# Pooled attention and a cosine-gated feed-forward: one unit order in the steady stages, and the cut of the last 128 rows

## The chip, the core and the metric

The kernel runs on one core of a Trainium2 chip. The metric is the device time of one execution in microseconds (us), as a median over runs. TensorE (PE, its weight loads listed apart as PEld) multiplies, VectorE (DVE) multiplies and copies out of PSUM, ScalarE (ACT) does exp, ln and sine, GpSimd (POOL) pools keys and values, SyncE (SP) issues DMAs.

## The reference

`q`, `k`, `v` are 8 x 8 x 576 x 64 (batch, heads, sequence, head size), `x` has 4608 tokens of 512, `w_in` is 512 x 2048, `w_out` 2048 x 512.

```python
k_p = k.reshape(B, H, 72, 8, D).mean(axis=3); v_p = likewise
attn = softmax(q @ k_p.T / sqrt(D))          # 72 pooled keys
x = (attn @ v_p) with heads side by side     # 4608 x 512
h = x @ w_in; g = h * cos(h); out = g @ w_out
```

## The kernel before

The feed-forward runs in nine stages `t` of 512 tokens. A stage is an **up phase** (64 matmuls of N=512 at L297, eight pairs of PSUM banks in turn, pair `fp` in `banks[fp % 3]`; ScalarE takes the cosine, VectorE multiplies into `g_sb`) and a **down phase** (64 matmuls of N=512 at L310 in four row blocks `ms` of 16, in `obanks[ms % 2]`; after each block `down_out` copies it to an `o_sb` buffer at L316 and issues two DMAs at L320). There are three `o_sb` buffers in rotation.

The attention of batch `b = t + 1` is done inside the down phase of stage `t`, by hand: a list `fill` of (place, step), where the step is issued ahead of down matmul number `place`. Engines work in the order of issue. A batch's 576 columns are cut into four units `us[0..3]` of 256 columns by four heads, and a rest, `REST`, of 64 columns and eight heads. A unit has two steps, each using one of the three pairs `banks[0..2]`:

- `scores` (matmuls at L211, then one exp on ScalarE at L218 into a tile `ex`); `two_` issues the matmuls of two units, then their exps.
- `values` (matmuls at L241; then on ScalarE two Ln of half the partitions each at L247 and one Exp at L248, which writes `inv`; then two multiplies on VectorE at L252, which write `xT`).

In the stages t = 1 to 6, which the text calls steady, `fill` places the four units of batch t+1 and the rest of batch t. The rest's columns are needed by the next up phase: its first matmul, at L297, reads `xT` and waits for the last multiply of L252. Before and after the ScalarE work of a down phase the activation tables are switched (L285, L288).

The last 128 rows (t = 8, ms = 3) are done by `last_chunk`, after everything else: 16 matmuls for each column piece, each piece copied and sent out by two DMAs of 64 rows, one from SP's queue and one from ACT's.

Of the kernel before, what the change touches and what calls it, by code (L numbers as in the profile page):

```python
# [19 lines left out]
def kernel(  # L20
# [9 lines left out]
    nc = tc.nc  # L30
    B, H, S, D = q.shape
# [15 lines left out]
    REST = (SEG[2], (0, H))  # L47
# [14 lines left out]
    w_out_sb = [wpool.tile([128, 4, d_model], BF16, name=f"w_out_sb{i}") for i in range(4)]  # L62
# [9 lines left out]
    banks = [psum.tile([128, 2, 512], FP32, name=f"bank{i}") for i in range(3)]  # L72
# [34 lines left out]
    def load_q(b):  # L107
        q_tile(b)
        load_even(staged["q", b], b, q)
# [60 lines left out]
    def k_transpose(b):  # L170
        nc.sync.dma_start_transpose(out=kk[b % 2], in_=kp2[b % 2].rearrange("p h s d -> p (h s d)"))
# [10 lines left out]
    def q_transpose(b):  # L182
        qT_tile(b)
        nc.sync.dma_start_transpose(out=att["qT", b], in_=q_flat(b))
# [10 lines left out]
    def ex_col(u, i):  # L195

        (c0, n), (h0, nh) = u
        return (i // 2 % 2 * (nh // 2) + i // 4 * 2 + i % 2) * n

    def scores(b, u, pair):  # L200
        scores_mm(b, u, pair)
        scores_exp(b, u, pair)

    def scores_mm(b, u, pair):
        (c0, n), (h0, nh) = u

        for i in [i + 2 * a for k in range(0, nh, 4) for i in (k, k + 1) for a in range(2)]:
            bank, c = divmod(ex_col(u, i), nh * n // 2)
            pj, hp = divmod(h0 + i, 2)
            g, r = divmod(ROW * pj + ORDER[c0 // 64], 2)  # L210
            nc.tensor.matmul(pair[:Sp, bank, c:c + n].rearrange("p (g n) -> p g n", n=64),  # L211
                             lhsT=kk[b % 2][half[r], h0 + i, 0:Sp],
                             rhs=att["qT", b][half[r], g:g + n // 64, hp * 64:hp * 64 + 64])

    def scores_exp(b, u, pair):
        (c0, n), (h0, nh) = u
        ex = asb.tile([Sp, 4 * 256], BF16, name="ex", tag="ex", bufs=EX)
        nc.scalar.activation(out=ex[:, 0:nh * n].rearrange("p (a n) -> p a n", a=2), in_=pair[:Sp, :, 0:nh * n // 2],  # L218
                             func=ACTF.Exp, scale=scale / POOL)
        att["ex", b, u] = ex  # L220

    def x_out(b, u, rows):
        (c0, n), (h0, nh) = u
        return xT[rows, h0 // 2:(h0 + nh) // 2, b * S + c0:b * S + c0 + n]

    def cols(x, u):
        n = u[0][1]
        return x[:, 0:n * u[1][1] // 2].rearrange("p (j n) -> p j n", n=n)

    def inverse_tile(w):  # L230
        lnc = asb.tile([128, 512], FP32, name="lnc", tag="lnc", bufs=1)
        inv = asb.tile([128, 512], FP32, name="inv", tag="inv", bufs=3)
        return lnc[:, 0:w], inv[:, 0:w]

    def values(b, u, pair, later=None):

        (c0, n), (h0, nh) = u
        ex = att.pop(("ex", b, u))
        for i in range(nh):
            pj, hp = divmod(h0 + i, 2)  # L240
            nc.tensor.matmul(pair[:, hp, (i // 2) * n:(i // 2 + 1) * n],  # L241
                             lhsT=vz[b % 2][:, pj, 2 * hp:2 * hp + 2, :].rearrange("p a d -> p (a d)"),
                             rhs=ex[:, ex_col(u, i):ex_col(u, i) + n])
        w = nh * n // 2
        lnc, inv = inverse_tile(w)
        for hp in range(2):
            nc.scalar.activation(out=lnc[half[1 - hp]], in_=pair[half[1 - hp], hp, 0:w], func=ACTF.Ln)  # L247
        nc.scalar.activation(out=inv, in_=lnc, func=ACTF.Exp, scale=-1.0)  # L248

        def mul():  # L250
            for hp in range(2):
                nc.vector.tensor_mul(out=x_out(b, u, half[hp]), in0=cols(pair[half[hp], hp, :], u),  # L252
                                     in1=cols(inv[half[1 - hp]], u))

        if later is None:
            mul()
        else:
            later.append(mul)
# [54 lines left out]
    def down_out(t, ms, ps, c0=0, queues=(nc.sync, nc.sync)):  # L313
        o = msb.tile([128, d_model], FP32, name="o_sb", tag="o_sb")
        n = ps.shape[1]
        nc.vector.tensor_copy(out=o[:, 0:n], in_=ps)  # L316
        rows_of = out.rearrange("(b p t) m -> b t p m", b=B, t=ROW)
        for i, rows in enumerate(half):
            b_, pos = divmod((t * TILE + ms * 128) // 64 + i, ROW)
            queues[i].dma_start(out=rows_of[b_, ORDER[pos], :, c0:c0 + n], in_=o[rows, 0:n])  # L320

    def last_chunk():

        t, ms = NT - 1, 3
        for hc in range(2):
            ps = banks[hc][:, 0, 0:256]
            for fc in range(FFCH):
                nc.tensor.matmul(ps, lhsT=g_sb[:, fc, ms * 128:(ms + 1) * 128],  # L328
                                 rhs=w_out_sb[fc // 4][:, fc % 4, hc * 256:(hc + 1) * 256],
                                 start=(fc == 0), stop=(fc == FFCH - 1))  # L330
            down_out(t, ms, ps, hc * 256, (nc.sync, nc.scalar))


    EX = 5
# [90 lines left out]
    for t in range(NT):  # L425
        b = t + 1
        for fp in range(FFCH // 2):
            up_mm(t, fp, 2 if t == 0 and fp < 2 else 0)
            between = ()
            if t == 0:  # L430
                if fp == 4:
                    puts = pool_k_mm(1, obanks[0], 0, 2), pool_k_mm(1, obanks[1], 2, 4)
                elif fp in (5, 6):
                    g0 = 9 * (fp - 5)
                    puts = q_transpose_mm(1, obanks[0], g0, g0 + 5), q_transpose_mm(1, obanks[1], g0 + 5, g0 + 9)
                if fp in (4, 5, 6):
                    puts[0](vec)
                    between = ((puts[1], act),)
            up_g(t, fp, between)
            if 0 < t and b < B:  # L440
                if fp == 0:
                    q_transpose(b)
                elif fp == 2:
                    k_transpose(b)
        mms = [(ms, fc) for ms in range(4) for fc in range(FFCH)]
        if t == 0:
            mms = [(ms, fc) for hm in range(2) for cg in range(4) for ms in range(2 * hm, 2 * hm + 2)
                   for fc in range(4 * cg, 4 * cg + 4)]


        def S_(n, bank):
            return lambda: scores(b, us[n], banks[bank])

        later = []

        def V_(n, bank, wait=None):
            return lambda: values(b, us[n], banks[bank], wait)

        fill = []
        if t < B:  # L460
            exp_tables()
            late = 0 < t and b < B
            fill = [(1, lambda: scores(t, REST, banks[2])), (12, lambda: values(t, REST, banks[2 if late else 1]))]
        if t == 0:
            fill[1:] = [(2, S_(0, 0)), (8, lambda: pool_v_mm(1, banks[1])), (8, lambda: values(t, REST, banks[2])),
                        (11, S_(1, 0)), (13, V_(0, 1)), (18, S_(2, 2)), (21, V_(1, 0, later)), (26, S_(3, 1)),
                        (32, lambda: later.pop()()), (32, V_(2, 2)), (40, V_(3, 0))]
        elif b < B:
            us = BY_TOKENS


            def two_(n, bank0, bank1):
                def go():
                    for mm in (scores_mm, scores_exp):
                        mm(b, us[n], banks[bank0])
                        mm(b, us[n + 1], banks[bank1])
                return go

            fill = [(4, two_(0, 2, 0)), (14, V_(0, 1)), (19, V_(1, 2)), (32, two_(2, 0, 1)), (36, fill[0][1]),
                    (38, V_(2, 0)), (41, V_(3, 1)), (45, fill[1][1])]  # L480
        fi = 0
        if t == NT - 1:
            mms = mms[:-FFCH]
        for n, (ms, fc) in enumerate(mms):
            while fi < len(fill) and fill[fi][0] <= n:
                fill[fi][1]()
                fi += 1
            down_mm(obanks[ms % 2], ms, fc)
            if fc == FFCH - 1:
                down_out(t, ms, obanks[ms % 2])  # L490
        if t < B:
            sin_tables()
        if 0 < t and b + 1 < B:

            nc.gpsimd.tensor_copy(out=gate, in_=kk[b % 2][0:1, 0, 0:1])  # L495
        if b + 1 < B:
            load_kv(b + 1, "k", k)
            load_q(b + 1)
            load_kv(b + 1, "v", v)
            pool_add(b + 1, "k")  # L500
            pool_add(b + 1, "v")
# [29 lines left out]
```

## Time and profile before

| | us |
|---|---|
| median of 3 runs (303.58 to 303.91) | 303.9 |
| the profiled execution | 303.9 |
| its span, first to last instruction | 302.1 |
| PE busy, 1798 matmuls | 294.0 |
| ACT busy | 206.8 |
| DVE busy | 172.3 |

The profiled execution's time is that of the median; 1.8 us of it lie around the span. The granted TensorE clock is full in all 40 slices of the span. The chain of work that ended last, followed back from the end, is 85% PE. Rows of the tail: `L328 PE MATMUL ... 128x256 bf16 x32` 273 ns each, `L316 DVE COPY o_sb<-bank 128x256` 424 ns, `L316 DVE COPY o_sb<-obank 128x512` 689 ns, DMAs of 64 KB 1.9 us (SP) and 2.2 us (ACT) from issue to landing, of 128 KB 2.4 us.

A time in the text such as 138.76 is in us from the span's start. A line of the timeline gives start, length, engine, source line, what is written and read, the count of merged instructions, and in brackets the idle time ahead of them and who ended it. In the chain a piece starts where the one before it ended, so a matmul's start there is up to 0.17 us later than the instruction's own.

### The profile page before, as it was taken

The page shows a single profiled execution, that of the slowest core. Times are in us where ns is not written, and L with a number is a line of the kernel's source. Part 1 is how long each engine was busy: PE and PEld are TensorE (multiplying, and loading weights), DVE is VectorE, ACT ScalarE, POOL GpSimd, SP SyncE. Part 2 cuts the span into 40 slices and gives each one's busy share as a digit, 9 for nine tenths or more (in the row PEclk, how much of TensorE's full clock was granted, in tenths as well). Part 3 has the DMA queues.
Part 4 walks back from the last instruction along what each step waited for, and adds up shares of the span by engine and source line. Part 5 has one row for each costly group of instructions (what it writes and reads, how often), then busy time and mean ns, then how long its engine had stood idle before and what let it go on. Part 6 is the DMA issues. An engine that isn't in the chain of part 4 may idle for free.

```text
span 302.1 us, 4605 instructions
## 1 busy us (share of the span) xinstructions
PE 294.0 (97%) x1798; PEld 141.6 (47%) x1798; DVE 172.3 (57%) x211; ACT 206.8 (68%) x255; POOL 129.8 (43%) x92
## 2 busy tenths in 40 slices
PE   8799999999999999999999999999999999999995
PEld 3545544445544454455444544454444544444444
DVE  5558636574566366645675566656574567425712
ACT  3887897469856986688768876788578956606500
POOL 8553007984973596349733991399100000000000
PEclk9999999999999999999999999999999999999999
DMA  7999999639546943695169617881900330131032
GB/s 152 201 207 206 208 204 196 152 44 174 109 113 105 167 92 70 123 171 113 44 132 161 115 36 162 129 141 36 167 5 1 71 69 0 27 79 35 0 71 71
DMA packets 44006, 32.92 MB, mean 109 GB/s; under 512 B 22096, under 2 KB 39248, under 8 KB 43984
## 3 DMA queue, kind: packets, MB, share of 16 engines
q0 software_dynamic: 19744, 18.07, 38.2%
q1 hardware_dynamic: 24080, 14.42, 21.0%
q8 instruction: 14, 0.23, 0.3%
q10 hardware_dynamic: 160, 0.13, 0.2%
q14 instruction: 8, 0.07, 0.1%
HBM read 36.70 MB, written 9.44 MB: 153 GB/s over the span
## 4 chain that ended last, share of the span: by engine, by line
PE 85%; DMA 10%; POOL 2%; ACT 1%; issue 0%; DVE 0%; POOLq 0%; ACTq 0%
PE obank L310 39%; PE bank L297 37%; DMA w_out_sb<-in_moe_w_out_dram 6%; PE bank L241 5%; DMA w_in_sb<-in_moe_w_in_dram 4%; PE bank L211 3%; PE bank L328 1%; POOL kv_st L84 1%; POOL kp L384 1%; POOL q_b L84 1%; ACT L285 0%; ACT cos L304 0%; ACT ex L218 0%; POOL identity masks.py:197 0%; DVE o_sb L316 0%
## 5 line engine op out<-in xcount | busy, mean ns | idle before, releaser
L310 PE MATMUL obank<-w_out_sb,g_sb 128*128 128x512 bf16 x560 | 132.5, 380 | 0.5 <-DMA w_out_sb<-in_moe_w_out_dram 0.5
L297 PE MATMUL bank<-xT,w_in_sb 128*128 128x512 bf16 x576 | 126.5, 379 | 0.0
L304 ACT ACTIVATE cos<-bank,half_pi 128x1024 f32<-128x1024 f32 x72 | 80.0, 1113 | 63.3 <-PE bank L297 63.3
L307 DVE TENSOR_TENSOR g_sb<-bank,cos 128x1024 bf16<-128x1024 f32 x72 | 88.1, 1225 | 48.2 <-ACT cos L304 48.2
L297 PEld LDWEIGHTS <-w_in_sb 128*128 128x128 bf16 x576 | 55.5, 98 | 68.6 <-DVE xT L252 2.5
L310 PEld LDWEIGHTS <-g_sb 128*128 128x128 bf16 x560 | 52.2, 97 | 56.9 <-issue 3.7
L252 DVE TENSOR_TENSOR xT<-bank,inv 64x512 bf16<-64x512 f32 (+1 forms) x72 | 45.3, 629 | 50.1 <-ACT inv L248 49.2
L141 POOL TENSOR_TENSOR kv_st<-kv_st 72x2048 f32<-72x2048 bf16 x12 | 48.7, 4056 | 35.2 <-DMA kv_st<-in_k_dram 35.2
L247 ACT ACTIVATE lnc<-bank 64x512 f32<-64x512 f32 (+1 forms) x72 | 39.2, 544 | 2.9 <-PE bank L241 1.3
L218 ACT ACTIVATE ex<-bank 72x1024 bf16<-72x1024 f32 (+1 forms) x40 | 35.0, 928 | 5.3 <-PE bank L211 5.2
L316 DVE COPY o_sb<-obank 128x512 f32<-128x512 f32 x35 | 23.6, 689 | 16.8 <-PE obank L310 16.2
L142 POOL TENSOR_TENSOR kv_st<-kv_st 72x1024 f32<-72x1024 f32 x12 | 28.2, 2348 | 1.0
L248 ACT ACTIVATE inv<-lnc 128x512 f32<-128x512 f32 (+1 forms) x36 | 21.0, 583 | 1.1
L241 PE MATMUL bank<-ex,vz 72*128 72x256 bf16 (+1 forms) x176 | 20.0, 243 | 0.2 <-ACT ex L218 0.2
L241 PEld LDWEIGHTS <-vz 72*128 72x128 bf16 x176 | 13.7, 97 | 9.9 <-issue 0.6
L145 POOL TENSOR_TENSOR kp<-kv_st 72x512 bf16<-72x512 f32 x12 | 14.9, 1264 | 0.5
L211 PE MATMUL bank<-qT,kk 64*72 64x256 bf16 (+1 forms) x192 | 13.3, 252 | 1.1 <-ACT qT L193 0.5
L211 PEld LDWEIGHTS <-kk 64*72 64x72 bf16 x192 | 7.6, 110 | 11.9 <-issue 8.1
L285 ACT ACT_TABLE_LOAD x9 | 11.5, 1283 | 0.9 <-PEq L515 0.7
L288 ACT ACT_TABLE_LOAD x9 | 11.5, 1283 | 0.2
L495 POOL COPY gate<-kk 1x1 bf16<-1x1 bf16 x5 | 0.9, 180 | 24.7 <-DMA kk<-kp 24.7
L84 POOL DMA_DIRECT2D q_b<-in_q_dram x10 | 7.7, 773 | 2.7 <-DMA w_in_sb<-in_moe_w_in_dram 1.4
(55 smaller groups left out, 89.8 us busy)
## 6 DMA issues: line engine op xcount, KB each, us to landing
out_dram<-o_sb SPq DMA_DIRECT2D x70, 128.0 KB, 2.4
kv_st<-in_v_dram POOLq DMA_DIRECT2D x8, 576.0 KB, 13.0
kv_st<-in_k_dram POOLq DMA_DIRECT2D x7, 576.0 KB, 7.7
q_b<-in_q_dram POOLq DMA_DIRECT2D x6, 576.0 KB, 9.9
w_in_sb<-in_moe_w_in_dram POOLq DMA_DIRECT2D x4, 512.0 KB, 13.7
w_out_sb<-in_moe_w_out_dram POOLq DMA_DIRECT2D x4, 512.0 KB, 18.4
q_b<-in_q_dram POOLq DMA_DIRECT2D x4, 288.0 KB, 12.1
g_sb<-in_k_dram SPq DMA_DIRECT2D x1, 576.0 KB, 3.5
```

The lines of the kernel that those rows point to most:

```text
L141: add(out=s, in0=x[:, :, 0:4, :], in1=x[:, :, 4:8, :], op=ADD)
L142: add(out=s[:, :, 0:2, :], in0=s[:, :, 0:2, :], in1=s[:, :, 2:4, :], op=ADD)
L211: nc.tensor.matmul(pair[:Sp, bank, c:c + n].rearrange("p (g n) -> p g n", n=64), lhsT=kk[b % 2][half[r], h0 + i, 0:Sp], rhs=att["qT", b][h ...
L218: nc.scalar.activation(out=ex[:, 0:nh * n].rearrange("p (a n) -> p a n", a=2), in_=pair[:Sp, :, 0:nh * n // 2], func=ACTF.Exp, scale=scale ...
L241: nc.tensor.matmul(pair[:, hp, (i // 2) * n:(i // 2 + 1) * n], lhsT=vz[b % 2][:, pj, 2 * hp:2 * hp + 2, :].rearrange("p a d -> p (a d)"), ...
L247: nc.scalar.activation(out=lnc[half[1 - hp]], in_=pair[half[1 - hp], hp, 0:w], func=ACTF.Ln)
L252: nc.vector.tensor_mul(out=x_out(b, u, half[hp]), in0=cols(pair[half[hp], hp, :], u), in1=cols(inv[half[1 - hp]], u))
L297: nc.tensor.matmul(h[:, j, :], lhsT=w_in_sb[fc // 4][:, ki, (fc % 4) * 128:(fc % 4 + 1) * 128], rhs=xT[:, ki, t * TILE:(t + 1) * TILE], st ...
L304: nc.scalar.activation(out=cos, in_=h, func=ACTF.Sin, bias=half_pi[:, :1])
L307: nc.vector.tensor_mul(out=g_sb[:, 2 * fp:2 * fp + 2, :], in0=h, in1=cos)
L310: nc.tensor.matmul(o, lhsT=g_sb[:, fc, ms * 128:(ms + 1) * 128], rhs=w_out_sb[fc // 4][:, fc % 4, :], start=(fc == 0), stop=(fc == FFCH - 1))
L316: nc.vector.tensor_copy(out=o[:, 0:n], in_=ps)
```

## The change

Two places. In `last_chunk` the 512 columns go in pieces of 256, 128 and 128, into `banks[0..2]`, in place of two of 256. In the steady stages the second pair of scores goes from place 32 to 31, the values of unit 2 from place 38 (pair 0) to 37 (pair 2), those of unit 3 stay at 41 (pair 0 in place of 1), the scores of the rest go from place 36 (pair 2), ahead of both, to 42 (pair 1), behind both, and the rest's values from 45 (pair 2) to 54 (pair 1). The stages 0, 7 and 8 issue what they did.

```diff
-        for hc in range(2):
-            ps = banks[hc][:, 0, 0:256]
+        for i, (c0, n) in enumerate(((0, 256), (256, 128), (384, 128))):
+            ps = banks[i][:, 0, 0:n]
             for fc in range(FFCH):
                 nc.tensor.matmul(ps, lhsT=g_sb[:, fc, ms * 128:(ms + 1) * 128],
-                                 rhs=w_out_sb[fc // 4][:, fc % 4, hc * 256:(hc + 1) * 256],
+                                 rhs=w_out_sb[fc // 4][:, fc % 4, c0:c0 + n],
                                  start=(fc == 0), stop=(fc == FFCH - 1))
-            down_out(t, ms, ps, hc * 256, (nc.sync, nc.scalar))
+            down_out(t, ms, ps, c0, (nc.sync, nc.scalar))
...
-            late = 0 < t and b < B
-            fill = [(1, lambda: scores(t, REST, banks[2])), (12, lambda: values(t, REST, banks[2 if late else 1]))]
+            fill = [(1, lambda: scores(t, REST, banks[1 if 0 < t and b < B else 2])), (12, lambda: values(t, REST, banks[1]))]
...
-            fill = [(4, two_(0, 2, 0)), (14, V_(0, 1)), (19, V_(1, 2)), (32, two_(2, 0, 1)), (36, fill[0][1]),
-                    (38, V_(2, 0)), (41, V_(3, 1)), (45, fill[1][1])]
+            fill = [(4, two_(0, 2, 0)), (14, V_(0, 1)), (19, V_(1, 2)), (31, two_(2, 0, 1)), (37, V_(2, 2)),
+                    (41, V_(3, 0)), (42, fill[0][1]), (54, fill[1][1])]
```

## The prediction

> **What bounds the kernel now.** PE is busy for 294.0 of 302.1 us at the full clock, so only PE's waits and the ends of the span can give or take time. I read first the waits of the weight loads over the whole span, since a waiting matmul's load waits ahead of it.
>
> ```profile
> PEld L297 <- DVE xT L252: 2.5, 6, 0.4
> ```
>
> Six times (the six steady stages) the first up matmul's load ends its idle time on VectorE's last multiply into `xT`. This is the only wait at the joint from a down phase to the next up phase, and it is there before the change. I take the stage t=3 (130.30 to 147.80); the other five repeat it. From the timeline of the joint, VectorE and the weight load:
>
> ```profile
> 145.39 2.28 DVE L252 TENSOR_TENSOR xT<-bank,inv 64x512 bf16<-64x512 f32 x4 [0.50 <-ACT inv L248]
> 147.72 0.11 PEld L297 LDWEIGHTS <-w_in_sb 128*128 128x128 bf16 x2 [0.41 <-DVE xT L252]
> ```
>
> The multiplies of unit 3 and of the rest end at 147.67, the load starts 0.05 later. The last down matmul starts at 147.43 in the same timeline; at 0.216 a matmul (19 in 4.10 below) the up phase could start at 147.64. So before loses 0.08 in each of six stages. Now the chain in that stage, PE's own order:
>
> ```profile
> 138.76 0.56 PE bank L211 x8
> 139.31 0.97 PE obank L310 x4
> 140.28 0.26 PE bank L211 x8
> 140.54 0.54 PE obank L310 x2
> 141.07 0.44 PE bank L241 x4
> ...
> 143.47 0.23 PE bank L241 x8
> 143.70 4.10 PE obank L310 x19
> ```
>
> Places 32 (scores of units 2 and 3), 36 (scores of the rest), 38 (values of unit 2), and 45 (values of the rest), with 19 matmuls, 4.10 us, left behind the last one. And ScalarE beside it:
>
> ```profile
> 139.14 2.41 ACT L218 ACTIVATE ex<-bank 72x1024 bf16<-72x1024 f32 x3 [0.68 <-PE bank L211]
> 141.61 1.19 ACT L247 ACTIVATE lnc<-bank 64x512 f32<-64x512 f32 x2
> 142.84 0.63 ACT L248 ACTIVATE inv<-lnc 128x512 f32<-128x512 f32 x1
> 143.50 1.20 ACT L247 ACTIVATE lnc<-bank 64x512 f32<-64x512 f32 x2
> 144.72 0.63 ACT L248 ACTIVATE inv<-lnc 128x512 f32<-128x512 f32 x1
> 145.39 0.77 ACT L247 ACTIVATE lnc<-bank 64x256 f32<-64x256 f32 x2
> 146.19 0.42 ACT L248 ACTIVATE inv<-lnc 128x256 f32<-128x256 f32 x1
> ```
>
> ScalarE has no pause over 0.06 from 139.14 to 146.61. The rest's values were ready at 143.70, yet their Ln starts at 145.39: the joint is set by ScalarE's and then VectorE's queue, not by PE.
>
> **The change, steady stages.** The amount of work is the same on every engine; only order and places move. PE's sum is thus unchanged, about 147.6 at the joint if nothing waits. What moves on ScalarE:
>
> Second scores one place earlier: exps start 0.22 earlier, at 138.92. The two of units 2 and 3 alone take 1.93 (the first pair of the same stage, same form, took 1.93 at 132.76), to 140.85.
>
> Values of unit 2 at place 37: scores now start at 138.54 in the chain, 0.56, then six matmuls (four took 0.97 right behind scores, two more 0.43), so 140.50, and their product ends 0.44 later, at 140.94. Ln follows 0.04 later (in stage 7 below: product over at 259.45, Ln at 259.49), at 140.98. ScalarE so idles 0.13, which before the rest's exp filled. A unit's Ln and Exp take 1.89 up to the next Ln (141.61 to 143.50), so unit 3 starts at 142.87 and its Exp is over 1.85 later, at 144.72.
>
> The rest's exp is now behind these two. Where an exp follows an Exp of `inv` that it doesn't depend on, it starts 0.10 ahead of that one's end (stage 0: 44.35 with 0.63, next exp at 44.88). So 144.62, with 0.59 alone: over at 145.21.
>
> From there everything is serial: product, Ln, Exp, multiply, load. The trace has this very chain by itself, in stage 7, where the rest is done alone:
>
> ```profile
> 258.41 0.59 ACT L218 ACTIVATE ex<-bank 72x512 bf16<-72x512 f32 x1
> 259.06 0.39 PE L241 MATMUL bank<-ex,vz 72*128 72x64 bf16 x8 [0.16 <-ACT ex L218]
> 259.49 0.77 ACT L247 ACTIVATE lnc<-bank 64x256 f32<-64x256 f32 x2 [0.48 <-PE bank L241]
> 260.28 0.42 ACT L248 ACTIVATE inv<-lnc 128x256 f32<-128x256 f32 x1
> 260.73 0.86 DVE L252 TENSOR_TENSOR xT<-bank,inv 64x256 bf16<-64x256 f32 x2 [2.38 <-ACT inv L248]
> ```
>
> Exp over at 259.00, multiplies over at 261.59: 2.59. So 145.21 + 2.59 + 0.05 = 147.85 for the first up load, against 147.72: **0.13 later in each of six stages, 0.78 in all**. PE would then wait some 0.24 at the joint where it waits 0.08 now. Nothing else is queued there to cover it: PE works in order, the up phase's other matmuls stand behind the first, and ScalarE and VectorE have over 1 us idle until the next cosine.
>
> Waits that the change could add on the way. (a) PE at place 54: the product's own start is 0.17 ahead of the chain's 145.41, so 145.24, and the exp ends at 145.21 plus 0.05 to be seen: 0.02. It is no extra, being on the same chain; behind it stand the last ten down matmuls, which end before 147.85 anyway. (b) PE at place 37 into pair 2, which unit 1's multiplies must have left. These end at 140.14 (138.75 plus 1.39 in VectorE's timeline), the product starts at 140.33. Free by 0.14 after 0.05 of signalling; were VectorE 0.2 late, PE would lose that difference there and unit 2's Ln with it, 0.06 a stage. (c) Pair 0 at place 41 and pair 1 at 42 were last read by exps over at 140.85, needed at 141.6 and later: free. (d) VectorE must copy row block 2 ahead of the rest's multiplies: unit 3's multiplies run from 144.75 to 146.14, the copy of 0.69 to 146.86, the rest's Exp is over at 146.91. Hidden by 0.05; without that cover, a delay counts fully. (e) SP: the output DMAs of block 2 go out some 1.5 us earlier and q's transpose behind them no later; POOL's write of `vz` at 148.14 comes after the last product that reads it (145.6 now). The next transposes that overwrite `qT` and `kk` are issued past 150. All are free.
>
> Bounds per stage: if the rest's exp can't start ahead of the Exp's end, add 0.13, 0.26 in all (six: 1.6); if signals and starts are all as quick as the shortest seen, 0.08 (six: 0.5).
>
> **The change, tail.** Products: now 32 at a spacing of 0.109 (from 3.66 us for 32 of 0.273). After: 16 of these and 32 of N=128. The trace has full 128x128 loads with N=128 in the transposes by matmul:
>
> ```profile
> 7.28 0.44 PE L192 MATMUL bank<-identity,q_b 128*128 128x128 bf16 x5
> ```
>
> Five within 0.44, one lasting 0.22: spacing 0.056. So 16 x 0.109 + 32 x 0.056 = 3.54 against 3.49; the last one is shorter by 0.05: the end of PE stays within 0.02. The rule against this is in the Trainium skill, "TensorE: Matmul & The Clock Gate", section on the back-to-back issue gap: with a weight load for each matmul it gives about 81 ns at N=128. By it the 32 would be an estimated 2.6 us and the tail 0.8 longer. It also gives 131 ns at N=512, where this trace has 216, so I go by the trace's row.
>
> Last copy: 128x512 took 0.69 and 128x256 0.42, so 128x128 about 0.29 (64x144 took 0.30): 0.13 less. But it is the third piece, and of three `o_sb` buffers it takes that of row block 2, whose second DMA is issued at 296.12 and lands 2.4 later, at 298.5. Before, the last copy took block 1's buffer and started at 298.38 right behind PE. So the copy waits to about 298.58 and ends near 298.87, against 298.80: 0.07 later. Without that wait it would be 0.13 earlier. The last two DMAs carry 32 KB in place of 64; from 128 to 64 KB the landing came down from 2.4 to 1.9 or 2.2, so another 0.15 less (0 to 0.3). Tail: 0.07 - 0.15 = -0.08, bounds -0.35 and +0.1.
>
> **Sum.** 303.9 + 0.78 - 0.08 = 304.6. About 0.2% (0.6 us) is what a measurement of this kernel can tell from no change, so 303.3 and 304.5 are the borders, and the forecast lies just beyond the upper one.
>
> **The rivals.**
> Same: the joint costs only the lower bound, 0.08, and the tail gains its 0.35, so 303.9 + 0.5 - 0.35 = 304.05. For it: the whole steady price hangs on differences of 0.1 us. Against: the serial 2.59 is measured as one piece. 0.29.
> Faster: PE no longer waits at the joint, because moving the second scores forward lets the last chain end ahead of PE. It gives back 0.08 in six stages, and with the tail's 0.35 comes to 303.1. It decides at an end of the rest's exp before 147.64 - 0.05 - 2.59 = 145.00; I have 145.21, and ScalarE's 0.13 of idle ahead of unit 2 doesn't make that up. 0.08.
> Slower by more: the rest's exp without the overlap (1.6), or cover (b) or (d) gone (0.06 to 0.1 a stage more). With the tail at +0.1 this ends at 305.2 to 305.6. 0.15.
> That the change doesn't do what it says is no case here: the engines work in the order of issue, and that is what it edits.
>
> **How the numbers follow.** The forecast itself, 304.5 to 305.1, has 0.48, so slower is 0.48 + 0.15 = 0.63, same 0.29, faster 0.08. Range: 304.0 (just below the same case's time) to 305.4 (inside the slow rival) leaves out some 2 in 10.
>
> **What would show it.** In the changed profile: the same row, the up phase's load waiting for `xT` six times, its idle time each 0.13 to 0.16 larger; in ScalarE's timeline the rest's exp behind unit 3's Exp, ending some 2.6 us ahead of the joint; a steady stage 0.13 longer than the 31.41 between two stages' first up matmuls (116.39 to 147.80); the last copy waiting for a DMA of `o_sb`, not for PE. I am wrong if the joint shows no wait, if values at place 37 or 54 stop PE by 0.1 or more, or if L328's N=128 matmuls are spaced by 0.08.

## The result, and the profile after

The changed kernel takes 304.9 us (304.77 to 305.42, 4 runs) against 303.81 before: a ratio of 1.004, 95% interval 1.0023 to 1.0058. It is slower, as forecast, by 1.1 us, where the forecast of 304.6 lay 0.7 above its 303.9, and within the range. Some runs of most kernels here, the one before included, take 3 to 5 us more than its others, so the intervals of the experiments are wide and a ratio need not be that of the two medians. The profiled execution took 304.85 with a span of 303.1, one us more than before's.

In the trace a steady stage, from one first up matmul to the next, lasts 31.62 in place of 31.41 in all six, 1.27 together. The last chunk, from its first matmul to the end, lasts 7.38 in place of 7.41, which is no more than the scatter between profiles: two-piece chunks took 7.41, 7.38 and 7.39 (before, `steady_only`, `values54`), three-piece ones 7.38, 7.39, 7.42 and 7.36 (after, `tail_only`, `values50`, `lnc2`). What is missing to the 0.98 by which the span grew lies ahead of the change: the first up phase of the steady stages starts at 53.25 in place of 53.50. That start lay between 53.1 and 54.3 in the profiles of this study (58.0 in that of `tail_4buf`), with no regard to what was edited.

The chain that ended last, followed back, has changed its make-up (page after, shares of the span by engine):

```profile
PE 80%; DMA 10%; ACT 3%; POOL 2%; issue 2%; DVE 1%; SPq 0%; DVEq 0%; ACTq 0%; POOLq 0%
```

ScalarE had 1% of it before. It does no more work than it did (206.8 us busy in both); more of that work now lies on the chain. Where it lies is seen in the chain of the same stage t=3 (start, length, what), here from the second scores on:

```profile
138.71 0.56 PE bank L211 x8
139.27 1.40 PE obank L310 x6
140.67 0.44 PE bank L241 x4
...
142.63 0.26 PE bank L211 x8
142.89 2.69 PE obank L310 x12
145.58 0.30 PE bank L241 x8
145.88 0.02 issue
145.90 0.02 ACTq L247
145.92 0.04 issue
145.96 0.38 ACT lnc L247
146.35 0.39 ACT lnc L247
146.76 0.43 ACT inv L248
...
147.64 0.44 DVE xT L252
148.12 1.89 PE bank L297 x8
```

Before, this stretch was PE's own from end to end. Now the chain leaves PE at the rest's values (145.58), goes through ScalarE and VectorE and comes back at 148.12, while PE's last ten down matmuls run beside it. The chain puts the time ahead of the rest's values down to PE, because the last down matmul's record is still running there. From start to start PE stands still for 0.05 at that place: the product starts 0.267 behind the down matmul ahead of it (0.216 without a wait) and 0.05 behind the end of the rest's exp. The product in PE's own timeline, then ScalarE's timeline of that stretch:

```profile
145.47 0.39 PE L241 MATMUL bank<-ex,vz 72*128 72x64 bf16 x8
```
```profile
139.09 1.93 ACT L218 ACTIVATE ex<-bank 72x1024 bf16<-72x1024 f32 x2 [0.46 <-PE bank L211]
141.20 1.19 ACT L247 ACTIVATE lnc<-bank 64x512 f32<-64x512 f32 x2 [0.17 <-PE bank L241]
142.42 0.63 ACT L248 ACTIVATE inv<-lnc 128x512 f32<-128x512 f32 x1
143.08 1.19 ACT L247 ACTIVATE lnc<-bank 64x512 f32<-64x512 f32 x2
144.31 0.63 ACT L248 ACTIVATE inv<-lnc 128x512 f32<-128x512 f32 x1
144.85 0.57 ACT L218 ACTIVATE ex<-bank 72x512 bf16<-72x512 f32 x1
145.96 0.77 ACT L247 ACTIVATE lnc<-bank 64x256 f32<-64x256 f32 x2 [0.54 <-PE bank L241]
146.76 0.42 ACT L248 ACTIVATE inv<-lnc 128x256 f32<-128x256 f32 x1
```

Two idle times have come in: 0.17 ahead of unit 2's Ln, 0.54 behind the rest's exp. VectorE's and the weight load's lines at the joint:

```profile
146.39 0.69 DVE L316 COPY o_sb<-obank 128x512 f32<-128x512 f32 x1
147.21 0.86 DVE L252 TENSOR_TENSOR xT<-bank,inv 64x256 bf16<-64x256 f32 x2
```
```profile
147.65 0.10 PEld L297 LDWEIGHTS <-w_in_sb 128*128 128x128 bf16 x1
148.12 0.10 PEld L297 LDWEIGHTS <-w_in_sb 128*128 128x128 bf16 x1 [0.38 <-issue]
```

The first up weight load no longer waits for `xT`; it is done at 147.75 and the matmul behind it waits to 148.12. From the last down matmul's start to the first up matmul's are 0.475 in place of 0.297, so of the 0.21 a stage PE spends 0.18 more at the joint, with the 0.05 at place 54 beside it (the up phase ahead is some 0.01 shorter). The trace lists what each instruction waits for: in the kernel before, the first up matmul had two semaphores, VectorE's held by its weight load and ScalarE's by itself; in the changed kernel it has VectorE's alone, held by the matmul, and the load is free to go ahead. The view of waits that carried the prediction therefore lost its row; in its place stands

```profile
PEld L297 <- issue: 2.6, 8, 0.4
```

which names nobody. The delay is found by the chain, or from start to start, not by this view.

The tail, in order of time, matmuls and copies:

```profile
295.69 3.70 PE L328 MATMUL bank<-w_out_sb,g_sb 128*128 128x256 bf16 x48
298.53 0.29 DVE L316 COPY o_sb<-bank 128x128 f32<-128x128 f32 x1 [0.47 <-PE bank L328]
299.62 0.29 DVE L316 COPY o_sb<-bank 128x128 f32<-128x128 f32 x1 [0.79 <-DMA out_dram<-o_sb]
```

The last copy before, and the landing of the small DMAs after (from the view of DMAs):

```profile
298.38 0.42 DVE L316 COPY o_sb<-bank 128x256 f32<-128x256 f32 x1 [1.32 <-PE bank L328]
```
```profile
out_dram<-o_sb SPq DMA_DIRECT2D x2, 32.0 KB, 1.8
out_dram<-o_sb ACTq DMA_DIRECT2D x2, 32.0 KB, 2.1
```

The products take 3.70 for 48 matmuls (the row names the form of the first): 16 spacings of 0.109, 31 of 0.056, and the last one's own 0.22. The third copy waits for a DMA of `o_sb`, where the last copy before waited for PE.

### The profile page after: what moved, and what is told of

Its sections match the earlier page's. It is cut to its first block, busy times and chain, and to the rows that moved or that the text cites. A ratio compares the mean times of both kernels' runs of the same rounds, so it can differ in the third digit from the quotient of the medians.

```text
span 303.1 us, 4638 instructions
## 1 busy us (share of the span) xinstructions
PE 294.6 (97%) x1814; PEld 142.0 (47%) x1814; DVE 173.0 (57%) x212; ACT 206.8 (68%) x255; POOL 129.8 (43%) x92
## 4 chain that ended last, share of the span: by engine, by line
PE 80%; DMA 10%; ACT 3%; POOL 2%; issue 2%; DVE 1%; SPq 0%; DVEq 0%; ACTq 0%; POOLq 0%
PE bank L297 37%; PE obank L310 35%; DMA w_out_sb<-in_moe_w_out_dram 6%; PE bank L241 5%; DMA w_in_sb<-in_moe_w_in_dram 4%; PE bank L211 3%; ACT lnc L247 2%; DVE xT L252 1%; ACT inv L248 1%; DMA out_dram<-o_sb 1%; POOL kv_st L84 1%; POOL kp L384 1%; POOL q_b L84 1%; ACT L285 0%; ACT cos L304 0%
## 5 line engine op out<-in xcount | busy, mean ns | idle before, releaser
L247 ACT ACTIVATE lnc<-bank 64x512 f32<-64x512 f32 (+1 forms) x72 | 39.1, 544 | 6.6 <-PE bank L241 5.6
```

## The experiments

**The steady stages alone.**

```diff
 # the changed kernel, with last_chunk as before
-        for i, (c0, n) in enumerate(((0, 256), (256, 128), (384, 128))):
+        for hc in range(2):
...
```

> Only the steady stages changed, the last rows in two pieces of 256 as before. Theory (the joint: the first up load waits for the rest's multiplies, 0.21 a stage more): the six steady stages 31.62 each between first up matmuls in place of 31.41, some 1.2 to 1.3 us over the kernel before, so 305.0 to 305.1 by a median of 303.8. Rival (the third column piece with its copy waiting for a DMA is what costs): no more than 0.3 us over the kernel before.

Measured: 305.14 against 303.81 us, ratio 1.0036 (1.0005 to 1.0068). The six stages are 31.63 each. Its chain at the joint is the changed kernel's:

```profile
147.96 0.44 DVE xT L252
148.44 0.81 PE bank L297 x3
```

The steady stages alone cost what the whole change costs.

**The tail alone.**

```diff
 # the kernel before, with last_chunk from the change
-        for hc in range(2):
+        for i, (c0, n) in enumerate(((0, 256), (256, 128), (384, 128))):
...
```

> Only the last rows in three pieces, the steady stages as before. Theory: -0.06 us (from the first matmul of the last chunk to the end 7.35 in place of 7.41), the same as before within what can be measured; the last copy waits for block 2's DMA by some 0.2 us behind PE's end. Rival: +0.8 us or more, the cost of the whole change.

Measured: 303.81 against 303.81 us, ratio 1.002 (0.9983 to 1.0057). The interval alone does not rule out the rival's 0.8 us; the trace does: 7.39 from the first matmul of the chunk to the end, 7.41 before, and stages of 31.41 or 31.42. The 0.06 that the theory expected to gain are not seen either.

**One place moved, the order kept.**

```diff
 # the kernel before
-                    (38, V_(2, 0)), (41, V_(3, 1)), (45, fill[1][1])]
+                    (38, V_(2, 0)), (41, V_(3, 1)), (54, fill[1][1])]
```

> The kernel before with one number changed: the rest's values at place 54 in place of 45; the rest's scores and exp stay ahead of the values of units 2 and 3. Theory (ScalarE's and VectorE's order sets the joint, not PE's place alone): here unit 3's Exp is over only at 145.35 of the stage as before, and VectorE's copy of row block 2 now stands ahead of the rest's multiplies, so these start at about 147.5 and end at 148.3: the joint 0.6 later a stage, 3.5 to 4 us in all, more than the whole change. Rival (the place 54 alone makes the delay, whatever the order): the same +0.2 a stage as in the changed kernel, 1.3 us in all.

Measured: 308.08 against 303.81, ratio 1.0145 (1.0097 to 1.0192); stages of 32.13 or 32.14, 0.73 more than before (0.6 was expected). VectorE's timeline:

```profile
146.92 1.39 DVE L252 TENSOR_TENSOR xT<-bank,inv 64x512 bf16<-64x512 f32 x2 [0.50 <-ACT inv L248]
148.34 0.69 DVE L316 COPY o_sb<-obank 128x512 f32<-128x512 f32 x1
149.06 0.86 DVE L252 TENSOR_TENSOR xT<-bank,inv 64x256 bf16<-64x256 f32 x2
```

Unit 3's multiplies, the copy of row block 2 and the rest's multiplies follow each other without a pause, and the first up matmul starts at 149.98. The rest's Exp was over at 148.49, so the copy holds the multiplies up by 0.54. Place 54 behind the old order puts the copy on the path; the change's own order avoids this, since unit 3's multiplies are done 0.6 earlier in the stage there. So the place has no price of its own: it depends on what ScalarE and VectorE still have queued.

**The same values earlier, the new order kept.**

```diff
 # the changed kernel
-                    (41, V_(3, 0)), (42, fill[0][1]), (54, fill[1][1])]
+                    (41, V_(3, 0)), (42, fill[0][1]), (50, fill[1][1])]
```

> The changed kernel with one number changed: the rest's values at place 50 in place of 54, their exp still behind unit 3's Exp. Theory (ScalarE's order makes the exp late): PE now reaches the values some 0.9 ahead of the exp and stands still with 14 down matmuls behind it; the joint comes at about 148.5 of the stage in place of 147.95, a steady stage near 32.2 in place of 31.62, 3.4 us over the changed kernel. Rival (place 54 is simply too late): four places earlier brings the joint forward, a stage of 31.4 to 31.5, about 1 us under the changed kernel.

Measured: 308.69 against 303.69 us, ratio 1.0179 (1.0122 to 1.0235); stages of 32.23. The chain:

```profile
145.63 0.63 ACT inv L248
146.26 0.49 ACT ex L218
146.75 0.04 issue
146.79 0.39 PE bank L241 x8
147.19 2.38 PE obank L310 x11
```

PE now stands still for 0.91 until the rest's exp is over (1.13 from start to start), and the joint itself has no wait (0.216 from start to start). The exp, and not the place, is what makes the values late; at 54 PE stopped for 0.05, so with the other steps where they are no earlier place can be had without a longer stop.

**Less to wait for on ScalarE.**

```diff
 # the changed kernel
-        lnc = asb.tile([128, 512], FP32, name="lnc", tag="lnc", bufs=1)
+        lnc = asb.tile([128, 512], FP32, name="lnc", tag="lnc", bufs=2)
```

> The changed kernel with two buffers for lnc in place of one, so that a Ln does not wait for ScalarE's own Exp before it. Theory (of the 0.21 a stage some 0.1 are ScalarE's separate waits ahead of a Ln with two semaphores to wait for, 0.085 to 0.1 from product to Ln in place of 0.04): the rest's Ln starts 0.04 behind its product and unit 3's Ln some 0.1 earlier; a stage of 31.50 to 31.54, 0.5 to 0.7 us under the changed kernel. Rival (the 0.2 is the order alone, signalling has no part in it): 31.62 as in the changed kernel.

Measured: 304.25 us against 303.69, ratio 1.0009 (0.9987 to 1.0032), stages of 31.51 or 31.52. ScalarE's timeline, and the product on PE:

```profile
145.57 0.57 ACT L218 ACTIVATE ex<-bank 72x512 bf16<-72x512 f32 x1
146.64 0.77 ACT L247 ACTIVATE lnc<-bank 64x256 f32<-64x256 f32 x2 [0.49 <-PE bank L241]
```
```profile
146.21 0.40 PE L241 MATMUL bank<-ex,vz 72*128 72x64 bf16 x8
```

The rest's Ln starts 0.04 behind the end of its product, in the changed kernel 0.10 (145.86 to 145.96); its separate semaphore instruction (`ACTq L247` in the chain above) is gone. The exp ends 0.05 earlier in the stage, because unit 2's Ln, too, starts 0.04 behind its product (141.90 to 141.93) in place of 0.09. Half of the change's cost per stage goes with these two. By the trace this is sure, since all six stages agree; the whole times alone (304.25, and 304.9 for the changed kernel measured at another time) say the same less sharply. One part of the expectation was missed: unit 3's Ln is 0.05 earlier, not 0.1, and still starts 0.03 behind the Exp before it.

**A free buffer for the third copy.**

```diff
 # the tail alone
-        o = msb.tile([128, d_model], FP32, name="o_sb", tag="o_sb")
+        o = msb.tile([128, d_model], FP32, name="o_sb", tag="o_sb", bufs=4)
```

> The last rows in three pieces and four o_sb buffers in place of three, the steady stages as before. Theory: the last copy no longer waits for block 2's DMA and starts right behind PE's end, 0.2 earlier than in the run with three buffers, so -0.25 us against the kernel before. Rival (the end hangs on the landing of earlier DMAs, not on the copy): no change against three buffers.

Measured: 303.63 us against 303.81, ratio 0.9993 (0.9965 to 1.0021), no difference that the runs can tell. In its profile the steady stages begin some 4.5 us late, so only its last chunk is read: 7.19, where the three-piece chunks with three buffers took 7.36 to 7.42; the next version, which has four buffers too, took 7.21. That is 0.2 less, by two profiles. The copies:

```profile
302.08 0.29 DVE L316 COPY o_sb<-bank 128x128 f32<-128x128 f32 x1 [0.47 <-PE bank L328]
302.97 0.29 DVE L316 COPY o_sb<-bank 128x128 f32<-128x128 f32 x1 [0.60 <-PE bank L328]
```

The last one now waits for PE, and starts 0.04 behind its end (302.94).

**A version that is faster than both.**

```diff
 # the kernel before, with the tail in three pieces and four o_sb buffers
-            fill = [(4, two_(0, 2, 0)), (14, V_(0, 1)), (19, V_(1, 2)), (32, two_(2, 0, 1)), (36, fill[0][1]),
-                    (38, V_(2, 0)), (41, V_(3, 1)), (45, fill[1][1])]
+            fill = [(4, two_(0, 2, 0)), (14, V_(0, 1)), (19, V_(1, 2)), (29, two_(2, 0, 1)), (34, V_(2, 0)),
+                    (37, V_(3, 1)), (38, fill[0][1]), (52, fill[1][1])]
```

> A version built from the readings: the kernel before with the second pair of scores at place 29 in place of 32, values of unit 2 at 34 (pair 0) and of unit 3 at 37 (pair 1), the rest's scores at 38 and its values at 52 (both pair 2), and the last rows in three pieces with four o_sb buffers. Theory: ScalarE's idle time ahead of the second exps is used, the rest's exp ends some 0.6 earlier than in the changed kernel, the joint is left to PE, a stage of 31.33 to 31.36, 0.3 to 0.5 us under the kernel before in the six stages and 0.2 at the tail: 0.5 to 0.7 us under it in all. Rival (PE meets a new wait at places 34 to 38, since the exps or the pairs aren't free yet): a stage of 31.5 or more, no faster than the kernel before.

Measured: 302.94 us against 303.69, ratio 0.9968 (0.9948 to 0.9988). The six stages are 31.32 each, the last chunk 7.21. ScalarE, VectorE and PE in t=3:

```profile
138.08 1.93 ACT L218 ACTIVATE ex<-bank 72x1024 bf16<-72x1024 f32 x2
143.69 0.57 ACT L218 ACTIVATE ex<-bank 72x512 bf16<-72x512 f32 x1
144.90 0.77 ACT L247 ACTIVATE lnc<-bank 64x256 f32<-64x256 f32 x2 [0.64 <-PE bank L241]
```
```profile
146.15 0.86 DVE L252 TENSOR_TENSOR xT<-bank,inv 64x256 bf16<-64x256 f32 x2 [0.23 <-ACT inv L248]
147.44 0.69 DVE L316 COPY o_sb<-obank 128x512 f32<-128x512 f32 x1 [0.43 <-PE obank L310]
```
```profile
147.23 0.59 PE L297 MATMUL bank<-xT,w_in_sb 128*128 128x512 bf16 x2
```

The rest's multiplies end at 147.01, the up phase starts at 147.23 with 0.216 from the last down matmul: PE's own pace. The second exps start without a pause on ScalarE (0.68 of idle time ahead of them before), with the order of the change; the rest's exp ends 0.57 earlier in the stage than in the changed kernel. Of the 0.75 us gained, 0.55 come from the six stages and 0.2 from the last chunk. Which of the moved places is needed for it, this run does not tell. Nor was the choice of bank pairs tested by itself; in the changed kernel no wait for a pair shows, since the products at places 37 and 41 start 0.216 behind the matmul ahead of them and the scores at 42 by the 0.31 of all scores.

## Why the prediction was right, point by point

**The bound.** That the joint hangs on ScalarE's and VectorE's queue, before the change already, was right: the last version removes that wait and gains 0.09 in each stage, the 0.08 and 0.01 more (the second up matmul followed the first by 0.226 before, by 0.216 there).

**The steady term was too small: 0.13 a stage forecast, 0.21 measured.** Stage t=3 of the changed kernel starts 0.17 later (down phase at 130.47 in the chain, 130.30 before), so 0.17 is taken off its times here. The exps of units 2 and 3 start at 138.92, as forecast to the hundredth, and unit 2's product ends at 140.94, as forecast. From there two sizes were off. First, Ln behind its product: the forecast took 0.04 from stage 7, where, by the trace, the Ln has one semaphore to wait for; unit 2's Ln started 0.09 behind (141.11 to 141.20). This carried over to the exp, over at 145.25 in place of 145.21. Second, the serial chain from the exp's end (145.42) to the first up matmul (148.12): 2.70 in place of 2.59 + 0.05, again with the rest's Ln 0.10 behind its product. The two make 0.10 at the joint, of which the stage shows 0.08. Such a Ln also waits for the Exp that last read `lnc`, and ScalarE executes a separate semaphore instruction ahead of it. The run with two `lnc` buffers shows that this belongs together: without it a stage costs 0.10 over before, not 0.21, and the forecast's 0.13 is about what it should have been. The step that failed is the reading of stage 7's chain as the same chain: the same work, but with fewer waits. That the whole still came within 0.3 us of the forecast is in part luck: 303.9 and the 1.27 of the six stages make 305.2, and the profile won 0.25 ahead of the first steady stage, where nothing was changed.

**The added waits.** (a) to (e) held. PE stopped 0.05 at place 54, where (a) had 0.02, and this is on the same chain. Unit 2's values started at 140.51 in place of the 140.33 + 0.17 forecast, with no stop. The copy of row block 2 was over at 147.08 and the rest's Exp at 147.18, a cover of 0.09 where (d) had 0.05. The run with place 54 in the old order shows what it costs without cover: 0.73 a stage. The wait at the joint was put at 0.24, though the prediction's own 147.85 and 147.64 give 0.21; it was 0.26.

**The tail: -0.08 forecast, nothing measured.** The difference of this pair of profiles, -0.03, is within the scatter given above; the account below is of this pair. N=128 matmuls are spaced by 0.056, so the trace's row was right. The 81 ns of the Trainium skill ("TensorE: Matmul & The Clock Gate", section on the back-to-back issue gap) are not seen in this kernel; the 56 ns that the same section gives by its formula for a single gap are. The sum of the products was off in one place: it counted a spacing behind the last matmul too, 0.109 before and 0.056 after, and so PE's end came 0.04 later in the chunk, not within 0.02. The copy waited 0.23 behind PE's end, against 0.2 forecast, and took 0.29 as forecast. From its end to the end of the span were 3.17, against 3.29: 0.13 less, forecast 0.15. The landing of 32 KB took 1.8 (SP) and 2.1 us (ACT), of 64 KB 1.9 and 2.2: the bytes matter little. The Trainium skill ("DMA: Bandwidth & Descriptors", section on the anatomy of one DMA, which is about GpSimd's path) puts the constant part of a DMA at about 2.0 us; these landings, from SP's and ACT's queues, lie within 0.2 us of it.

**What it said would be seen.** The stage was to be longer by 0.13 and was by 0.21; the exp ended 2.7 ahead of the joint, 2.6 forecast; the last copy waited for a DMA as forecast. The row of the weight loads was to grow and vanished, because the load went ahead of the wait: that a waiting matmul's load waits ahead of it, from which the prediction set out, held before the change and not after it.

**The rivals.** Not the same: that needed a joint at the lower bound of 0.08 a stage and 0.35 from the tail, and it was 0.21 and nothing. Not faster: the exp was to end before 145.00 for that, and did at 145.25. The case of much slower had its exp without overlap, which did not come: it started 0.09 ahead of the end of the Exp before it (144.85 against 144.31 + 0.63).

## What to carry to other kernels

When steps are moved along an engine that is hardly ever idle, add up the queues of the other engines from the moved step to the next joint: here PE's work in a steady stage never changed, and the cost came from when ScalarE, in its new order, got to the rest. Shift the start of the second engine's work into its idle time first, then move the late step; the same order that lost 0.21 a stage gains 0.09 with the second scores at place 29, three ahead of the old place, and the steps behind them moved up too. And take a chain measured elsewhere only with its waits, since an instruction that waits for two semaphores can start later than one that waits for one, here a Ln by 0.05 each time.

## What was not expected of the hardware

A Ln on ScalarE with two things to wait for started 0.09 to 0.10 us behind the later one, against 0.04 with a single one (stage 7, and the run with two `lnc` buffers). An Exp's successor starts 0.09 to 0.10 ahead of its end where nothing is shared (the rest's exp), but a Ln behind an Exp of `inv` kept 0.03 behind it even with `lnc` in two buffers; why is open.
